# SiLU as a half of g times (1 + tanh(g/2)): one activation on ScalarE and one more pass on VectorE

## The chip, the cores and the metric

The kernel runs on one core of one Trainium2 chip. The metric is the device time of one execution in microseconds (us). In what follows PE is TensorE (matmuls, with PEld for its weight loads), DVE is VectorE, ACT is ScalarE, POOL is GpSimd and SP issues the DMAs.

## The reference

Three stages follow each other. Attention works on 4 batches of 8 heads, 576 tokens and 64 columns a head; half of the heads see a local window of 32 tokens, half a strided pattern. Its output, 2304 tokens of 512 numbers, goes through a gated layer and then through a layer with three products of which the largest counts:

```
g = x @ w_gate                       # 512 -> 1536
silu = g * (1.0 / (1.0 + np.exp(-g)))
val = x @ w_val                      # 512 -> 1536
x = (silu * val) @ w_out             # 1536 -> 512
h = np.maximum(np.maximum(x @ w1, x @ w2), x @ w3)   # 512 -> 768
return h @ w_out2                    # 768 -> 512
```

The change touches only the line `silu`.

## The kernel before

Tokens lie along the free axis. The gated layer cuts the 2304 tokens into five column blocks `c` (480, 480, 448, 448 and 448 tokens) and the 1536 hidden columns into twelve pieces `f` of 128. One pair (c, f) is called a **slot** here, numbered s = 12 c + f from 0 to 59. In slot s the PE makes the gate product `ps_g` (12 matmuls, lines 503 to 505, function `linear`), then the value product `ps_v` (12 matmuls), and then the output product of slot s-1 (`emit_out`: 12 matmuls, or 4 slower ones, line 549, issued as 8, while c is 0). Most products are made of three matmuls, of the high and low halves of their operands.

Both `ps_g` and `ps_v` come from the PSUM pool `gv`, which has two buffers. So the gate product of slot s+1 writes the buffer that held the gate product of slot s, and may begin only when the last reader of `ps_g` of slot s is done. Before the change that reader is ACT (line 523). The value product of slot s+1 waits in the same way for the DVE product of slot s (line 530), which reads `ps_v`.

The product `ht` of line 530 is then split in a high half `hh` (ACT, line 135) and a low half `hl` (POOL, line 138), from which the next output product is made; while c is 0 it is used whole.

Between the slots other work is woven in. While c is 0 each slot loads, converts (lines 158 to 163) and splits (lines 135, 138) three pieces of the weights, and does a share of the attention of block c = 1: scores (303), masked maximum and softmax (311 to 321: the exponential is line 316), transposes (326), values (340, 345, 346), and units of strided attention done on DVE or POOL (415 to 440: exponential on line 425, sums on 418 and 440). While c is 1 to 3 each slot does a share of the attention of block c+1, with its products on POOL, and of the preparation of the last layer's weights (lines 161 to 163, 195 to 198, 206, 207). At the end of block c = 4 the y blocks of the last layer are loaded and prepared (lines 135, 138, 583 to 587).

The order of instructions on each engine is set when the program is built, by a scheduler that follows a simulated timeline; each engine then works through its own list in that order and waits where an operand is not there yet. The last layer (lines 599 on) begins about 566 us after the start and takes the rest of the span.

Of the kernel before, what the change touches and what calls it, by code (L numbers as in the profile page):

```python
# [11 lines left out]
AF = mybir.ActivationFunctionType  # L12
ALU = mybir.AluOpType
# [46 lines left out]
def tile_attention_swiglu_maxout(  # L60
# [18 lines left out]
    nc = tc.nc  # L79
# [38 lines left out]
    def width(c):  # L118
        return STRIDE * (ROWS[c + 1] - ROWS[c])
# [11 lines left out]
    def split(hi, lo, src, hi_eng, lo_eng):  # L131
        if hi_eng is nc.gpsimd:
            a = nc.gpsimd.tensor_scalar(hi, src, 1.0, 1.0, ALU.mult, ALU.mult)
        elif hi_eng is nc.scalar:
            a = nc.scalar.activation(hi, src, AF.Copy)  # L135
        else:
            a = nc.vector.tensor_copy(hi, src)
        return a.ins, lo_eng.tensor_tensor(lo, src, f32(hi), ALU.subtract).ins  # L138
# [368 lines left out]
    def linear(ps, w, x, n):  # L507
        xh, xl = x
        for k in range(NK):
            ks = slice(k * 128, (k + 1) * 128)  # L510
            product(ps, w[0][:, ks], w[1][:, ks], xh[:, k, :n], xl[:, k, :n], k == 0, k == NK - 1)
# [6 lines left out]
    def emit_gate(c, f):  # L518
        n = width(c)
        ps = gv.tile([128, 512], F32, name="ps_g", tag="gv")  # L520
        linear(ps[:, :n], wt["g", f], xt[c], n)
        t = h_p.tile([128, N], F32, name="ht", tag="ht" if c or f % 2 else "hh")[:, :n]
        nc.scalar.activation(t, ps[:, :n], AF.Silu)  # L523
        return t

    def emit_val(c, f, t):
        n = width(c)
        ps = gv.tile([128, 512], F32, name="ps_v", tag="gv")
        linear(ps[:, :n], wt["v", f], xt[c], n)
        m = nc.vector.tensor_tensor(t, ps[:, :n], t, ALU.mult).ins  # L530
        if c == 0:
            hs[c, f] = (t, t)
            return
        hh = h_p.tile([128, N], F32R, name="hh")[:, :n]
        hl = h_p.tile([128, N], F32R, name="hl")[:, :n]
        last_val[:] = [m, *split(hh, hl, t, nc.scalar, nc.gpsimd)]
        hs[c, f] = (hh, hl)
# [214 lines left out]
    if True:  # L752
# [32 lines left out]
        for s, (c, f) in enumerate(slots):  # L785
# [4 lines left out]
            if work:  # L790
                weight_step()
            t = emit_gate(c, f)
            if work:
                weight_step()
            emit_val(c, f, t)
            if work:
                weight_step()
# [167 lines left out]
```

## Time and profile before

| | before |
|---|---|
| median of 3 runs | 851.76 us (849.8 to 852.48) |
| the profiled execution's own time | 850.72 us |
| its span | 848.9 us |
| busy PE, PEld | 808.7 us (95%), 712.2 us (84%) |
| busy DVE, ACT, POOL | 519.3 us (61%), 374.4 us (44%), 408.7 us (48%) |
| mean granted TensorE clock | 0.986 |

Busy time is the time in which an engine had an instruction in work. For the PE it says little: matmuls are pipelined and their ends are modelled, so a PE that is 100% busy in a stretch can still be slowed. Where the profile shows idle PE time it also names what the PE waited for.

### The profile page before, as it was taken

Reading aid. Unit: us, or ns where it says so; the run is one execution under the profiler, and the core shown is the slowest. Engines: PE = TensorE matmul, PEld = TensorE weight load, DVE = VectorE, ACT = ScalarE, POOL = GpSimd, SP = SyncE. Lnnn points to the kernel's source line nnn. Section 1 sums busy time; section 2 is a strip of 40 time slices with the busy share of each in tenths; the row PEclk is TensorE's granted clock in tenths of the full one; section 3 lists DMA queues with packets and bytes.
Section 4 is the critical chain, followed back from the end, with each engine's and each line's share of the span. In section 5 each row is a group of like instructions: output and inputs, shape, how many; then the busy total and the mean of one; then the engine's idle time right before and its main releaser. Section 6 shows DMA issues by size and latency. Waiting matters only on the chain.

```text
span 848.9 us, 12625 instructions
## 1 busy us (share of the span) xinstructions
PE 808.7 (95%) x4392; PEld 712.2 (84%) x4392; DVE 519.3 (61%) x1028; ACT 374.4 (44%) x844; POOL 408.7 (48%) x355
## 2 busy tenths in 40 slices
PE   4699988989999999999998999999999999999997
PEld 3577665768888899989887999999999899989986
DVE  3889977886576778846889552543644254524340
ACT  4987677653545353645243233432244123512220
POOL 0586566876477869746788444430313021302110
PEclk9799998999999999999999999999999999999999
DMA  8779688986766699868677997579766385654502
GB/s 231 237 237 363 202 273 294 361 261 215 246 201 217 220 311 313 297 194 274 205 226 212 350 300 271 169 291 407 252 234 217 129 284 215 220 190 147 212 1 75
DMA packets 73915, 202.72 MB, mean 239 GB/s; under 512 B 8716, under 2 KB 38472, under 8 KB 70268
## 3 DMA queue, kind: packets, MB, share of 16 engines
q1 hardware_dynamic: 73852, 201.92, 69.8%
q8 instruction: 35, 0.57, 0.3%
q14 instruction: 28, 0.23, 0.1%
HBM read 160.21 MB, written 41.68 MB: 238 GB/s over the span
## 4 chain that ended last, share of the span: by engine, by line
PE 63%; DVE 7%; POOL 3%; DMA 2%; issue 2%; ACT 2%; SPq 0%; DVEq 0%; ACTq 0%; POOLq 0%
PE ps_a L611 13%; PE ps_z L684 8%; PE ps_c L611 7%; PE ps_v L503 3%; PE ps_g L503 3%; PE ps_y L505 3%; PE ps_v L505 3%; PE ps_g L504 3%; PE ps_b L611 3%; PE ps_v L504 3%; PE ps_y L504 3%; PE ps_y L503 3%; PE ps_g L505 3%; POOL pr L415 1%; DMA wr<-wsdr 1%
## 5 line engine op out<-in xcount | busy, mean ns | idle before, releaser
L138 POOL TENSOR_TENSOR hl<-t,hh 128x384 fp32r<-128x384 f32 x36 | 37.6, 1047 | 207.5 <-ACT hh L135 160.4
L503 PE MATMUL ps_g<-xh,wh_g 128*128 128x448 f32 (+1 forms) x240 | 94.4, 394 | 10.2 <-ACT ht L523 8.1
L611 PE MATMUL ps_a<-yhT,wr 128*128 128x384 f32 x324 | 94.4, 338 | 0.6 <-ACT s L625 0.6
L503 PE MATMUL ps_v<-xh,w_v 128*128 128x448 f32 (+1 forms) x240 | 90.5, 377 | 3.5 <-DVE ht L530 3.3
L138 POOL TENSOR_TENSOR hl<-ht,hh 128x448 fp32r<-128x448 f32 (+1 forms) x48 | 60.1, 1253 | 68.1 <-ACT hh L135 60.7
L504 PE MATMUL ps_g<-xl,wh_g 128*128 128x448 f32 (+1 forms) x240 | 90.7, 378 | 0.9 <-DVE xl L346 0.9
L505 PE MATMUL ps_g<-xh,wl_g 128*128 128x448 f32 (+1 forms) x240 | 90.2, 376 | 0.0
L505 PE MATMUL ps_v<-xh,w_v 128*128 128x448 f32 (+1 forms) x240 | 89.5, 373 | 0.0
L504 PE MATMUL ps_v<-xl,w_v 128*128 128x448 f32 (+1 forms) x240 | 89.2, 372 | 0.0
L625 ACT ACTIVATE s<-ps_a 128x384 f32<-128x384 f32 x81 | 39.4, 490 | 98.4 <-PE ps_a L611 98.2
L437 POOL TENSOR_TENSOR pr<-stv,stsc 128x832 f32<-128x832 f32 (+17 forms) x42 | 67.5, 1625 | 29.2 <-DVE stsc L430 13.4
L415 POOL TENSOR_TENSOR pr<-stk,stq 128x832 f32<-128x832 f32 (+17 forms) x42 | 70.9, 1708 | 9.0 <-DVE sto L440 7.3
L505 PE MATMUL ps_y<-hh,w_o 128*128 128x448 f32 (+1 forms) x192 | 71.4, 372 | 0.0
L504 PE MATMUL ps_y<-hl,w_o 128*128 128x448 f32 (+1 forms) x192 | 71.2, 371 | 0.0
L160 POOL TENSOR_SCALAR raw<-raw 128x512 f32<-128x512 f32 x60 | 54.1, 902 | 33.4 <-ACT w L158 15.9
L503 PE MATMUL ps_y<-hh,w_o 128*128 128x448 f32 (+1 forms) x192 | 68.2, 374 | 0.0
L135 ACT ACTIVATE hh<-ht 128x448 fp32r<-128x448 f32 (+1 forms) x48 | 28.0, 584 | 88.4 <-DVE ht L530 88.4
L684 PE MATMUL ps_z<-wo2t,hh 128*128 128x512 f32 x216 | 64.8, 392 | 0.9 <-ACT osb L693 0.7
L530 DVE TENSOR_TENSOR ht<-ps_v,ht 128x448 f32<-128x448 f32 (+1 forms) x60 | 37.9, 631 | 41.9 <-PE ps_v L505 25.8
L503 PEld LDWEIGHTS ps_g<-xh,wh_g 128*128 128x128 f32 x240 | 45.8, 191 | 18.6 <-ACT ht L523 10.0
L611 PEld LDWEIGHTS ps_a<-yhT,wr 128*128 128x128 f32 x324 | 59.7, 188 | 1.6 <-ACT s L625 1.0
L163 DVE CUSTOM_DVE_ANT_0 w<-w,q 128x1024 uint16<-128x1024 uint16 x60 | 54.1, 902 | 1.7
(138 smaller groups left out, 1982.4 us busy)
## 6 DMA issues: line engine op xcount, KB each, us to landing
wr<-wsdr SPq DMA_DIRECT2D x27, 1792.0 KB, 7.5
raw<-in_w_dram SPq DMA_DIRECT2D x60, 512.0 KB, 5.3
w_v<-wvdr SPq DMA_DIRECT2D x48, 512.0 KB, 4.7
w_o<-wodr SPq DMA_DIRECT2D x48, 512.0 KB, 4.8
wsdr<-whi SPq DMA_DIRECT2D x27, 256.0 KB, 4.0
wvdr<-w_v SPq DMA_DIRECT2D x12, 512.0 KB, 4.5
wodr<-w_o SPq DMA_DIRECT2D x12, 512.0 KB, 5.8
wsdr<-w SPq DMA_DIRECT2D x18, 256.0 KB, 4.1
```

Of the source, the lines that this page charges most:

```text
L138: return a.ins, lo_eng.tensor_tensor(lo, src, f32(hi), ALU.subtract).ins
L160: nc.gpsimd.tensor_scalar(f32(hi), f32(hi), -0.0, 1.0, ALU.mult, ALU.mult)
L163: nc.vector.tensor_tensor(w, w, q, ALU.add)
L415: eng.tensor_tensor(pv, self.k[:, 0:i + 1, :], self.q[:, r:r + 1, :].to_broadcast([128, i + 1, D]), ALU.mult)
L437: eng.tensor_tensor(pv, self.v[:, :, 0:i + 1], self.sc[:, r:r + 1, 0:i + 1].to_broadcast([128, D, i + 1]), ALU.mult)
L503: nc.tensor.matmul(ps, wh, xh, start=first, stop=False)
L504: nc.tensor.matmul(ps, wh, xl, start=False, stop=False)
L505: nc.tensor.matmul(ps, wl, xh, start=False, stop=last)
L530: m = nc.vector.tensor_tensor(t, ps[:, :n], t, ALU.mult).ins
L611: nc.tensor.matmul(ps, wts[:, c, a, ks], y[k][b], start=first and k == q == 0, stop=k == 1 and q == 2, skip_group_check=True,)
L625: nc.scalar.activation(s, self.a, AF.Copy)
L684: nc.tensor.matmul(z[j], a[:, ts], w[:, f, b], start=f == q == 0, stop=f == NF2 - 1 and q == 2)
```

## The change

The activation of line 523 becomes a tanh of half of the gate product. A new DVE instruction adds 1 to it and multiplies by the gate product, which it reads from PSUM. The product with `ps_v` takes in the factor 0.5.

```
         t = h_p.tile([128, N], F32, name="ht", tag="ht" if c or f % 2 else "hh")[:, :n]
-        nc.scalar.activation(t, ps[:, :n], AF.Silu)
+        nc.scalar.activation(t, ps[:, :n], AF.Tanh, scale=0.5)
+        nc.vector.scalar_tensor_tensor(t, t, 1.0, ps[:, :n], ALU.add, ALU.mult)
         return t
...
-        m = nc.vector.tensor_tensor(t, ps[:, :n], t, ALU.mult).ins
+        m = nc.vector.scalar_tensor_tensor(t, t, 0.5, ps[:, :n], ALU.mult, ALU.mult).ins
```

All lines behind the new one move down by one: the new DVE instruction is line 524, and the product that was line 530 is line 531. In the built program the instructions that load a table into ACT (ACT_TABLE_LOAD) go from 34 to 1, the one at the start. The scheduler also places other work a little differently. Three places follow, with the rows of the DVE list; `ht<-ps_v,ht` or `ht<-ht,ps_v` is the product with the value, `ht<-ht,ps_g` the new instruction.

First the DVE around the product of slot 5, in block c = 0 (`pr` and `sto` are strided attention, `w_...` weights under conversion). Before:

```order
L430 TENSOR_TENSOR stsc<-stsc,ssum 128x36
L437 TENSOR_TENSOR pr<-stv,stsc 128x1088
L437 TENSOR_TENSOR pr<-stv,stsc 128x1152
L162 SCALAR_TENSOR_TENSOR w_992<-w_992,raw 128x512
L440 TENSOR_REDUCE sto<-pr 128x64
L530 TENSOR_TENSOR ht<-ps_v,ht 128x480
L138 TENSOR_TENSOR w_v_999<-w_964,w_v_999 128x512
```

Now:

```order
L437 TENSOR_TENSOR pr<-stv,stsc 128x1088
L437 TENSOR_TENSOR pr<-stv,stsc 128x1152
L440 TENSOR_REDUCE sto<-pr 128x64
L524 SCALAR_TENSOR_TENSOR ht<-ht,ps_g 128x480
L138 TENSOR_TENSOR w_v_1002<-w_967,w_v_1002 128x512
L162 SCALAR_TENSOR_TENSOR w_995<-w_995,raw 128x512
L440 TENSOR_REDUCE sto<-pr 128x64
L346 TENSOR_TENSOR xl<-ps_a,xh 128x2x128
L531 SCALAR_TENSOR_TENSOR ht<-ht,ps_v 128x480
```

The new instruction of slot 5 stands behind the two long products of line 437 and a sum of line 440, about where the product stood; the product has moved four rows further back.

Then the DVE of slots 44 and 45, in block c = 3 (`s_...` are sums of weights of the last layer). Before:

```order
L195 TENSOR_TENSOR s_4658<-w_4651 128x256
L440 TENSOR_REDUCE sto<-pr 128x64
L196 TENSOR_TENSOR s_4658<-s_4658,w_4567 128x256
L198 TENSOR_TENSOR s_4659<-w_4567,s_4658 128x256
L530 TENSOR_TENSOR ht<-ps_v,ht 128x448
L440 TENSOR_REDUCE sto<-pr 128x64
L207 TENSOR_TENSOR w_4567<-w_4567,whi 128x512
L207 TENSOR_TENSOR s_4658<-s_4658,whi 128x512
L440 TENSOR_REDUCE sto<-pr 128x64 x2
L530 TENSOR_TENSOR ht<-ps_v,ht 128x448
```

Now:

```order
L524 SCALAR_TENSOR_TENSOR ht<-ht,ps_g 128x448
L195 TENSOR_TENSOR s_4702<-w_4695 128x256
L196 TENSOR_TENSOR s_4702<-s_4702,w_4610 128x256
L531 SCALAR_TENSOR_TENSOR ht<-ht,ps_v 128x448
L198 TENSOR_TENSOR s_4703<-w_4610,s_4702 128x256
L440 TENSOR_REDUCE sto<-pr 128x64 x2
L207 TENSOR_TENSOR w_4610<-w_4610,whi 128x512
L207 TENSOR_TENSOR s_4702<-s_4702,whi 128x512
L524 SCALAR_TENSOR_TENSOR ht<-ht,ps_g 128x448
L440 TENSOR_REDUCE sto<-pr 128x64
L531 SCALAR_TENSOR_TENSOR ht<-ht,ps_v 128x448
L440 TENSOR_REDUCE sto<-pr 128x64
```

The product of slot 44 has moved ahead of line 198; the new instruction of slot 45 stands where two sums of line 440, which were ahead of the product, are still to come.

Last the DVE of slots 57 and 58, near the end of block c = 4 (`yl`, `yh`, `rB`, `rT` are the y blocks). Before:

```order
L530 TENSOR_TENSOR ht<-ps_v,ht 128x448
L138 TENSOR_TENSOR ylB_5626<-rB_5608,yhB_5625 128x384
L138 TENSOR_TENSOR ylB_5630<-rB_5613,yhB_5629 128x384
L583 TENSOR_TENSOR rT_5618<-rB_5610,rB_5608 128x384
L138 TENSOR_TENSOR ylT_5638<-rT_5618,yhT_5637 128x384
L586 TENSOR_TENSOR rT_5619<-rB_5615,rT_5618 128x384
L138 TENSOR_TENSOR ylB_5650<-rB_5615,yhB_5649 128x384
L587 TENSOR_TENSOR rT_5620<-rB_5613,rT_5619 128x384
L138 TENSOR_TENSOR ylT_5642<-rB_5610,yhT_5641 128x384
L530 TENSOR_TENSOR ht<-ps_v,ht 128x448 x2
```

Now:

```order
L531 SCALAR_TENSOR_TENSOR ht<-ht,ps_v 128x448
L138 TENSOR_TENSOR ylB_5684<-rB_5666,yhB_5683 128x384
L138 TENSOR_TENSOR ylB_5688<-rB_5671,yhB_5687 128x384
L584 TENSOR_TENSOR rT_5676<-rB_5668,rB_5666 128x384
L587 TENSOR_TENSOR rT_5677<-rB_5673,rT_5676 128x384
L138 TENSOR_TENSOR ylT_5696<-rT_5676,yhT_5695 128x384
L588 TENSOR_TENSOR rT_5678<-rB_5671,rT_5677 128x384
L138 TENSOR_TENSOR ylB_5708<-rB_5673,yhB_5707 128x384
L524 SCALAR_TENSOR_TENSOR ht<-ht,ps_g 128x448
L138 TENSOR_TENSOR ylT_5700<-rB_5668,yhT_5699 128x384
L531 SCALAR_TENSOR_TENSOR ht<-ht,ps_v 128x448
```

The new instruction of slot 58 stands behind all of this work on the y blocks but one subtraction of line 138.

## Rows read from the trace of the kernel before

**Rows 1.** Table loads on ACT by line: busy us, mean ns; idle before, releaser.

```profile
L523 ACT ACT_TABLE_LOAD x17 | 21.8, 1283 | 2.4 <-PE ps_g L505 2.1
...
L425 ACT ACT_TABLE_LOAD x10 | 12.8, 1283 | 9.0 <-DVE stsc L424 8.8
...
L316 ACT ACT_TABLE_LOAD x7 | 9.0, 1283 | 0.8 <-PEq L952 0.7
```

**Rows 2.** What the PE waited for, 48 to 566 us: total, times, longest.

```profile
PE ps_g L503 <- ACT ht L523: 8.1, 3, 3.3
```

**Rows 3.** Blocks c = 0, 1: length, busy PE, PEld, DVE, ACT, POOL; PEclk, DMA, GB/s.

```profile
48.65:175.77 127.12, 121.24 (x579) 86.28 (x577) 109.08 (x200) 88.20 (x176) 85.11 (x77) 0.97 0.87 293
175.77:283.71 107.94, 104.19 (x579) 88.30 (x578) 73.58 (x165) 50.12 (x119) 76.39 (x66) 0.98 0.68 224
```

**Rows 4.** Timeline of slot 51: the activation and the next gate product.

```profile
500.82 0.55 ACT L523 ACTIVATE ht<-ps_g 128x448 f32<-128x448 f32 x1 [2.52 <-PE ps_g L505]
...
505.44 0.37 PE L503 MATMUL ps_g<-xh,wh_g 128*128 128x448 f32 x1
```

**Rows 5.** Busy time of the DVE alone in slots 3 to 6 (us, busy).

```profile
75.60:108.90 33.30, 33.00 (x60) 1.00 0.78 266
```

**Rows 6.** Timeline around slot 5's DVE product: start, us, engine, line.

```profile
97.42 0.52 PE L503 MATMUL ps_g<-xh,wh_g 128*128 128x480 f32 x1
...
100.53 0.64 DVE L530 TENSOR_TENSOR ht<-ps_v,ht 128x480 f32<-128x480 f32 x1
...
101.10 0.67 DVE L138 TENSOR_TENSOR w_v<-w,w_v 128x512 fp32r<-128x512 f32 x1
```

**Rows 7.** Timeline of slots 6 and 7: ACT, DVE and the next gate product.

```profile
116.70 0.17 DVE L319 TENSOR_SCALAR stat<-stat 128x4 f32<-128x4 f32 x1 [2.02 <-ACT sm L316]
...
119.64 1.28 ACT L523 ACT_TABLE_LOAD   x1
...
120.94 0.57 ACT L523 ACTIVATE ht<-ps_g 128x480 f32<-128x480 f32 x1
...
121.54 0.66 DVE L530 TENSOR_TENSOR ht<-ps_v,ht 128x480 f32<-128x480 f32 x1 [0.76 <-ACT ht L523]
...
121.56 0.49 PE L503 MATMUL ps_g<-xh,wh_g 128*128 128x480 f32 x1 [3.29 <-ACT ht L523]
```

**Rows 8.** Timeline of slot 13: ACT, DVE and the gate product of slot 14.

```profile
186.70 1.28 ACT L523 ACT_TABLE_LOAD   x1
186.71 1.95 DVE L319 TENSOR_SCALAR stat<-stat 128x4 f32<-128x4 f32 x1 [0.49 <-ACT sm L316]
...
188.61 0.77 PE L503 MATMUL ps_g<-xh,wh_g 128*128 128x480 f32 x1 [3.17 <-ACT ht L523]
...
188.80 0.66 DVE L530 TENSOR_TENSOR ht<-ps_v,ht 128x480 f32<-128x480 f32 x1
```

**Rows 9.** Timeline of slot 45: DVE, and the gate product of slot 46.

```profile
460.84 2.27 DVE L440 TENSOR_REDUCE sto<-pr 128x64 f32<-128x960 f32 x2
...
461.06 0.37 PE L503 MATMUL ps_g<-xh,wh_g 128*128 128x448 f32 x1
...
463.03 0.61 DVE L530 TENSOR_TENSOR ht<-ps_v,ht 128x448 f32<-128x448 f32 x1
```

**Rows 10.** Timeline of slot 58: DVE, gate and value product of slot 59.

```profile
556.57 0.37 PE L503 MATMUL ps_g<-xh,wh_g 128*128 128x448 f32 x1
...
558.10 0.55 DVE L138 TENSOR_TENSOR ylT<-rB,yhT 128x384 fp32r<-128x384 f32 x1
...
558.57 0.61 DVE L530 TENSOR_TENSOR ht<-ps_v,ht 128x448 f32<-128x448 f32 x1
...
559.24 0.47 PE L503 MATMUL ps_v<-xh,w_v 128*128 128x448 f32 x1
```

**Rows 11.** Two stretches after PE stalls (columns as rows 3; 0.66 and 0.83 are PEclk).

```profile
140.00:150.00 10.00, 9.65 (x26) 6.21 (x27) 7.21 (x23) 7.76 (x21) 6.21 (x7) 0.66 0.96 330
185.00:195.00 10.00, 6.83 (x26) 5.47 (x25) 7.23 (x9) 5.72 (x14) 8.80 (x8) 0.83 0.24 88
```

## The prediction

> **What bounds the kernel now.** I read the grouped instructions of ACT first. A function that is not in the table ACT holds costs a table load, and SiLU and the exponentials of attention push each other out: 34 loads of 1.283 us, 17 ahead of the activation of line 523 and 17 ahead of an exponential [rows 1]. That is 43.6 us of ACT, and the reader should ask at once who waits for ACT. The PE's waits answer: between 48 and 566 us it waited 8.1 us for the activation that frees `ps_g`, in three places, 3.3 us at most [rows 2]. So the 43.6 us are nearly all beside other work, and no more than about 8 us of them can come back in this way.
>
> Next the stretches. In block c = 0 the DVE is busy 109.08 of 127.12 us (86%) and ACT 88.20 (69%); in c = 1 the DVE has 73.58 of 107.94 us [rows 3]. The change takes work from the second of these engines and gives work to the first. The reader should see the margin too: in a quiet slot the activation ends at 501.37 us and the next gate product starts at 505.44, because the PE has the value product and an output product to do in between. So `ps_g` is free 4.07 us before it is needed [rows 4]. A new reader of `ps_g` costs nothing as long as it is done inside that margin.
>
> Then the timeline of the DVE where it is fullest: from 75.6 to 108.9 us, slots 3 to 6, it is busy 33.00 of 33.30 us [rows 5]. There the DVE, not the PE, paces the slots, and what is put on its list pushes all that stands behind it.
>
> **The change part by part.** *Removed:* 33 table loads, 42.3 us of ACT. Only those on the way to a wait count. *Unchanged:* the tanh is an activation of the same shape, and the product with the factor 0.5 is the old product with a constant more; I take both at the old length, since a constant adds no element (0 taken; 60 x 0.02 us, the difference between two such products in [rows 6, 7], as the other end). *Added:* 60 DVE instructions over 448 or 480 columns, one operand in PSUM and one in SBUF, the shape of the product of line 530. This operation on such operands has no row; the nearest is that product, 0.64 us long with the next DVE instruction starting 0.57 us after it [rows 6]. I take 0.57 us where more work is queued and 0.65 us where someone waits for the end; 60 of them are 34 us of DVE.
>
> *Moved:* the freeing of `ps_g`. Before, ACT did it; now the new DVE instruction does, and it waits in the DVE's list behind whatever the scheduler put there. Queued behind it are the product with `ps_v`, on which the split and the next output product hang, and the weight conversions. So in each slot two DVE instructions must be in time instead of one, and the first of them about one value product earlier. This is the wait that takes the place of the table loads. I go through the places where the DVE is late.
>
> *Slot 5.* Before, the product ran at 100.53 us behind the line 437 and 440 work, while the next gate product had already started at 97.42, since ACT had freed the buffer [rows 6]. In the new list the new instruction stands about where the product stood, with one conversion (line 162, some 1 us) moved behind it. New instructions of slots 3 and 4 push it by 2 x 0.57. So it starts near 100.53 - 1.0 + 1.1 = 100.6 and ends near 101.3: the gate product of slot 6 starts 3.9 us later than before.
>
> *Slot 7* gives most of that back. The gate product of slot 8 waited 3.29 us at 121.56 for the activation, behind a table load at 119.64 [rows 7]. The PE, 3.9 us later, uses up that wait and is 3.9 - 3.3 = 0.6 us later at slot 8. The DVE allows this: its list ran to 120.78 (121.54 less 0.76 of waiting), gets four new instructions (2.3 us) in the meantime and loses a 2.02 us wait for exponentials [rows 7], so its new instruction starts at about 121.0 and ends at 121.7, before the PE's 122.2. I take **+0.6**, bounds -3.3 (the DVE is never late) and +3.9 (the wait is not used up).
>
> *Slots 8 to 12.* Five new instructions, 2.9 us of DVE in a block where it is busy 86% [rows 3]. Between nothing and 2.9 us I take the half, **+1.4**.
>
> *Slot 13.* The gate product of slot 14 started at 188.61 after 3.17 us of waiting for the activation, behind the load at 186.70. That load goes. But in the new list the new instruction stands behind a scaling of the softmax (line 319) that took 1.95 us from 186.71, and the old product started behind it at 188.80 [rows 8]. The new one then ends at 188.80 + 0.65 = 189.45: **+0.8**. Bounds: -1.3 if that scaling takes a short 0.17 us as in [rows 7] (189.45 less 1.8 is 187.7, 0.9 us earlier than before, and a little less clock is lost) and +0.8.
>
> *Slots 44 and 45.* The DVE is a long list here; in the new order two sums of line 440, 2.27 us for both, have moved behind the new instruction of slot 45. The old product started at 463.03, so the new instruction starts at 463.03 - 2.27 + 0.57 (that of slot 44) = 461.3 and ends at 461.95, against a gate product that started at 461.06 [rows 9]: **+0.9**. Bounds: 0 and +3.2 (none of the sums helps).
>
> *Slot 58.* The old product started at 558.57; of what was ahead of it only one subtraction (0.47 us to the next start) has moved behind the new instruction. That ends at 558.57 - 0.47 + 0.61 = 558.7 against a gate product that started at 556.57. The value product of slot 59, which followed at 559.24, comes at 558.7 + 2.67 (a gate product, between these two rows) = 561.4 [rows 10]: **+2.1**, bounds 0 and +2.6.
>
> *Everywhere else* the new instruction lies inside the margin of 4 us [rows 4]. The last layer is not touched.
>
> The sum is 0.6 + 1.4 + 0.8 + 0.9 + 2.1 = 5.8 us on the profiled execution's own 850.72 us, so **856.5 us**. The median of the runs shown is 851.76, 1.04 above that execution; a median of the changed kernel may stand as far above 856.5, which the range holds.
>
> *A rule against this change.* The new instruction starts its successor 0.57 us after its own start, a little under its length [rows 6]; I counted that. The Trainium skill (VectorE: DVE Perf Modes, Rules for kernel authors) says of chained DVE work to minimize the number of operations, since each pays its pipeline drain whatever is fused. By the same page's figure for a two-operand fp32 operation, (N + 151)/0.96 ns, an estimate is 0.66 us a piece at 480 columns, which would make the half of five instructions 1.6 instead of 1.4 us.
>
> **The rivals.** *Relief, faster.* The waits for the activation go and the DVE is always in time. It needs the new instruction to end within 4 us of the gate product in slots 5, 44, 45 and 58 too, where the old list says 2 to 4 us later [rows 6, 9, 10]; the order could help if real waits for exponentials on the DVE (2.02 us at 116.70, [rows 7]) shrink by the loads ahead of them. Price: 8.1 us [rows 2] and the low clock behind the stall at 185 us, (1 - 0.83) x 10 = 1.7 us [rows 11]: 850.7 - 9.8 = 841 us; with half of it 846. It decides from the point where the new instruction of slot 5 ends before 97.4.
> What a load costs bears on this rival. In the rows the activation follows 1.30 us after the load's start [rows 7]. The Trainium skill (ScalarE: Activation LUTs, What ACT_TABLE_LOAD costs) adds a drain and gives about 2.66 us for every switch, and names exp and tanh as one set. By it the 33 switches would be 88 us of ACT; the trace does not show such a drain, and the waits, which are measured, stay what they are.
>
> *Even.* Half of the waits come back and half of the new ones come: 850.7 + (5.8 - 8.1)/2 = 849.6. For it speaks that slot 5's delay is paid out of a wait that goes; against it that slot 58 has no wait to give back.
>
> *The DVE becomes the bound of c = 0.* All twelve instructions lie on the path, 12 x 0.57 = 6.8 us in place of 0.6 + 1.4; with the other terms (3.8) and one more stall of about 3.4 us of low clock as at 140 to 150 us, (1 - 0.66) x 10 [rows 11], 864.7. For it speaks 86% of busy time, against it the 18 us in which the DVE of that block still waits [rows 3].
>
> That the loads stay is excluded by the built program, which has one.
>
> **How the numbers follow.** About 0.3%, 2.6 us, is what a measurement of this kernel can tell from no change. The forecast (853.4 to 860) has 0.42, the DVE bound (860 to 867) 0.13, both slower: 0.55. Even (848 to 853.3) has 0.22. Relief (841 to 848) has 0.23. The range from 846 to 866 leaves out the better half of relief and little above: 0.15. The likeliest case's own range is 853.4 to 860.
>
> **What would show it.** ACT has one table load and is some 42 us less busy; the DVE some 34 us more. The PE's waits for ACT at its gate products are gone, and waits for the new DVE instruction (`ht`, line 524) stand in their place: about 4 us at slot 6, others near slots 14, 46 and 59. Blocks c = 1 and c = 2 change by less than 2 us. If instead the PE has no wait at line 503 for the DVE, my step on slot 5 is wrong, and relief is right; if c = 0 is 7 us or more longer, the DVE has become its bound. Waits of the PE for other engines, weights above all, would make me wrong in a way that is not in the cases.

## The result, and the profile after

The changed kernel takes 859.21 us (median of 5 runs, 857.32 to 861.69), the kernel before, run beside it, 849.8 us (848.37 to 852.48). The recorded ratio is 1.0086, with an interval from 1.0058 to 1.0114 (these two medians alone give 1.011, within it): it became slower. The two profiled executions took 859.57 and 850.72 us, 8.85 us apart; that is the difference which the steps below divide up.

The page's busy times of the changed kernel, with its span ahead:

```profile
span 857.7 us, 12675 instructions
...
PE 813.2 (95%) x4392; PEld 714.6 (83%) x4392; DVE 557.1 (65%) x1088; ACT 331.2 (39%) x811; POOL 408.2 (48%) x355
```

ACT is 43 us less busy (374.4 before) and the DVE 38 us more (519.3 before). The groups by line answer to [rows 1], first on ACT:

```profile
L316 ACT ACT_TABLE_LOAD x1 | 1.3, 1283 | 0.7 <-PEq L953 0.7
...
L531 DVE SCALAR_TENSOR_TENSOR ht<-ht,ps_v 128x448 f32<-128x448 f32 (+1 forms) x60 | 37.7, 629 | 20.7 <-PE ps_v L505 19.3
L524 DVE SCALAR_TENSOR_TENSOR ht<-ht,ps_g 128x448 f32<-128x448 f32 (+1 forms) x60 | 37.6, 626 | 33.3 <-ACT ht L523 33.3
```

One load is left of 34. The new instruction takes 626 ns, as long as the product beside it. What the PE waited for between 48 and 575 us answers to [rows 2]:

```profile
PE ps_g L503 <- DVE ht L524: 14.2, 9, 4.3
PE ps_a L303 <- DVE xl L346: 2.4, 2, 2.1
PE ps_v L503 <- DVE ht L531: 2.4, 2, 1.7
PE ps_a L326 <- DVE sm L321: 1.3, 1, 1.3
```

No gate product waits for ACT any more. In place of 8.1 us for the activation stand 14.2 us for the new DVE instruction, in nine places. The timeline shows the two waits in the full stretch of the DVE (81.25 us, for the new instruction of slot 3, and 85.83 us, for the product of slot 3), and the places of the forecast, which answer to [rows 6] to [rows 10]:

```profile
79.29 1.34 DVE L415 TENSOR_TENSOR pr<-stk,stq 128x1152 f32<-128x1152 f32 x1
80.56 0.64 DVE L524 SCALAR_TENSOR_TENSOR ht<-ht,ps_g 128x480 f32<-128x480 f32 x1
...
81.25 0.49 PE L503 MATMUL ps_g<-xh,wh_g 128*128 128x480 f32 x1 [1.55 <-DVE ht L524]
...
85.83 0.48 PE L503 MATMUL ps_v<-xh,w_v 128*128 128x480 f32 x1 [1.68 <-DVE ht L531]
...
97.25 0.55 ACT L523 ACTIVATE ht<-ps_g 128x480 f32<-128x480 f32 x1
...
100.85 0.64 DVE L524 SCALAR_TENSOR_TENSOR ht<-ht,ps_g 128x480 f32<-128x480 f32 x1
...
101.29 0.45 PE L340 MATMUL ps_a<-loct 96*64 96x64 f32 x8
...
101.68 0.48 PE L503 MATMUL ps_g<-xh,wh_g 128*128 128x480 f32 x1
...
120.01 0.17 DVE L319 TENSOR_SCALAR stat<-stat 128x4 f32<-128x4 f32 x1 [0.96 <-ACT sm L316]
...
122.75 0.64 DVE L524 SCALAR_TENSOR_TENSOR ht<-ht,ps_g 128x480 f32<-128x480 f32 x1
...
122.97 0.60 PE L326 MATMUL ps_a<-cst,sm 128*60 128x128 f32 x4 [1.30 <-DVE sm L321]
...
123.44 0.48 PE L503 MATMUL ps_g<-xh,wh_g 128*128 128x480 f32 x1
...
188.67 2.33 POOL L437 TENSOR_TENSOR pr<-stv,stsc 128x1088 f32<-128x1088 f32 x1 [0.37 <-DVE sto L440]
...
189.14 1.88 DVE L319 TENSOR_SCALAR stat<-stat 128x4 f32<-128x4 f32 x1 [0.55 <-ACT sm L316]
...
191.16 0.64 DVE L524 SCALAR_TENSOR_TENSOR ht<-ht,ps_g 128x480 f32<-128x480 f32 x1
...
191.85 0.77 PE L503 MATMUL ps_g<-xh,wh_g 128*128 128x480 f32 x1 [4.27 <-DVE ht L524]
...
457.66 0.47 PE L503 MATMUL ps_v<-xh,w_v 128*128 128x448 f32 x1 [0.70 <-DVE ht L531]
...
465.42 0.47 PE L503 MATMUL ps_g<-xh,wh_g 128*128 128x448 f32 x1 [2.42 <-DVE ht L524]
...
561.73 1.37 DVE L587 TENSOR_TENSOR rT<-rB,rT 128x384 f32<-128x384 f32 x1 [2.13 <-DMA rB<-ydr]
...
565.23 0.61 DVE L524 SCALAR_TENSOR_TENSOR ht<-ht,ps_g 128x448 f32<-128x448 f32 x1
...
565.89 0.47 PE L503 MATMUL ps_g<-xh,wh_g 128*128 128x448 f32 x1 [1.84 <-DVE ht L524]
```

Each time the new instruction is late on the DVE. In slot 5 ACT is done with `ps_g` at 97.80 us, but the new instruction starts 3.05 us later, behind the strided attention on the DVE. The gate product of slot 6 starts 0.19 us after its end, but the row shows no wait there: the PE had attention's products (line 340) to make until 101.74 us, so its own work and the release ended within 0.3 us of each other. In slot 58 the instruction is held up by work on a y block whose DMA the DVE itself waited 2.13 us for: a transfer that has nothing to do with `ps_g` now delays its release.

A wait of the PE can have a second price. These are two stretches from a gate product to the next, slot 14 and slot 46, of the kernel before (length, busy times, then the granted clock as a share of 2.4 GHz):

```profile
188.61:196.60 7.99, 7.99 (x32) 6.82 (x33) 4.70 (x7) 2.92 (x5) 5.62 (x6) 0.81 0.01 4
461.06:467.10 6.04, 6.04 (x32) 5.45 (x31) 4.60 (x6) 2.54 (x6) 6.04 (x4) 1.00 1.04 327
```

and of the changed one:

```profile
191.85:201.00 9.15, 9.15 (x36) 7.73 (x37) 5.27 (x6) 3.25 (x6) 5.12 (x5) 0.74 0.03 5
465.42:472.90 7.48, 7.48 (x30) 6.58 (x31) 6.36 (x9) 2.79 (x6) 7.48 (x6) 0.77 0.83 249
```

The PE is busy throughout in all four, but behind the waits of 4.27 and 2.42 us it ran part of the time at the lower level, 1.2 GHz, and the slots took 1.16 and 1.44 us longer than before. Not all of the 1.16 is clock: the changed order has 36 matmuls in that slot instead of 32, and at full clock the two would be 0.74 x 9.15 = 6.8 and 0.81 x 7.99 = 6.5 us, which leaves 0.9 us for the clock. Nor has every wait this price: behind the 1.84 us at slot 59 the granted clock is 1.00.

### The profile page after: what moved, and what is told of

It reads as the page before. It is cut to its first block, busy times and chain, and to the rows that moved or that the text cites. A ratio compares the mean times of both kernels' runs of the same rounds, so it can differ in the third digit from the quotient of the medians.

```text
span 857.7 us, 12675 instructions
## 1 busy us (share of the span) xinstructions
PE 813.2 (95%) x4392; PEld 714.6 (83%) x4392; DVE 557.1 (65%) x1088; ACT 331.2 (39%) x811; POOL 408.2 (48%) x355
## 4 chain that ended last, share of the span: by engine, by line
PE 60%; DVE 10%; POOL 4%; DMA 2%; issue 2%; ACT 1%; SPq 0%; DVEq 0%; POOLq 0%; ACTq 0%
PE ps_a L612 13%; PE ps_z L685 8%; PE ps_c L612 7%; PE ps_g L503 3%; PE ps_g L504 3%; PE ps_g L505 3%; PE ps_b L612 3%; PE ps_v L503 3%; PE ps_v L505 3%; PE ps_v L504 3%; PE ps_y L503 3%; PE ps_y L504 3%; PE ps_y L505 3%; POOL pr L415 3%; DVE stsc L418 1%
## 5 line engine op out<-in xcount | busy, mean ns | idle before, releaser
L503 PE MATMUL ps_g<-xh,wh_g 128*128 128x448 f32 (+1 forms) x240 | 95.9, 400 | 16.4 <-DVE ht L524 14.2
L503 PE MATMUL ps_v<-xh,w_v 128*128 128x448 f32 (+1 forms) x240 | 90.8, 378 | 2.4 <-DVE ht L531 2.4
L505 PE MATMUL ps_v<-xh,w_v 128*128 128x448 f32 (+1 forms) x240 | 91.1, 380 | 0.0
L505 PE MATMUL ps_y<-hh,w_o 128*128 128x448 f32 (+1 forms) x192 | 71.2, 371 | 0.0
L503 PE MATMUL ps_y<-hh,w_o 128*128 128x448 f32 (+1 forms) x192 | 64.9, 375 | 0.0
L524 DVE SCALAR_TENSOR_TENSOR ht<-ht,ps_g 128x448 f32<-128x448 f32 (+1 forms) x60 | 37.6, 626 | 33.3 <-ACT ht L523 33.3
L523 ACT ACTIVATE ht<-ps_g 128x448 f32<-128x448 f32 (+1 forms) x60 | 32.9, 549 | 67.4 <-PE ps_g L505 60.5
```

Of the source, the lines that this page charges most:

```text
L503: nc.tensor.matmul(ps, wh, xh, start=first, stop=False)
L505: nc.tensor.matmul(ps, wl, xh, start=False, stop=last)
L523: nc.scalar.activation(t, ps[:, :n], AF.Tanh, scale=0.5)
L524: nc.vector.scalar_tensor_tensor(t, t, 1.0, ps[:, :n], ALU.add, ALU.mult)
```

## The experiments

The theory, A, is that of the prediction: the loss comes from the place of the release, `ps_g` being freed from a place far back in the DVE's list. The rival, B, is that 37.6 us more work on the DVE cost the time wherever they stand. Beside both stands the question what the 33 loads were worth. Each kernel is compared with the kernel before on the same chip (851.5 to 851.9 us there; the changed kernel would be at about 859.0 by its ratio, 7.3 us above it, with an interval from 4.9 to 9.7).

**The two halves of the change.** The first kernel keeps the tanh and leaves out the new instruction, the second keeps it but goes back to SiLU as the function.

```diff
         nc.scalar.activation(t, ps[:, :n], AF.Tanh, scale=0.5)
-        nc.vector.scalar_tensor_tensor(t, t, 1.0, ps[:, :n], ALU.add, ALU.mult)
```

> The tanh stands alone: the new VectorE instruction is left out, so the hidden layer becomes tanh(g/2) times half of the value instead of SiLU times the value. The table loads are gone and ScalarE frees ps_g as before the change. Theory A (the loss comes from ps_g being freed late, behind the list of the DVE): only the relief is left, so 841 to 847 us, with the PE's 8.1 us of waits for the activation down to under 2 us. Theory B (the loss comes from 38 us more DVE work): the same 841 to 847 us. Theory C (the loss comes from the order into which the scheduler put everything else once the loads' instruction was another): no gain, 850 us or more.

```diff
-        nc.scalar.activation(t, ps[:, :n], AF.Tanh, scale=0.5)
+        nc.scalar.activation(t, ps[:, :n], AF.Silu)
         nc.vector.scalar_tensor_tensor(t, t, 1.0, ps[:, :n], ALU.add, ALU.mult)
```

> SiLU on ScalarE with its 34 table loads stays, and the new DVE instruction is there all the same, reading ps_g (the hidden layer becomes (SiLU(g)+1) times g/2 times the value). Theory A: both the loads and the DVE's list now lie between the gate product and the freeing of ps_g; where the list is late the loads add little, so 860 to 865 us, less than after plus the whole relief. Theory B: cost and relief simply add, so after plus what the kernel with the tanh alone gains, some 864 to 868 us.

The tanh alone took 847.74 us, ratio 0.9945 (0.9925 to 0.9965), just above the 841 to 847 that A and B both expected. Apart from the loads it lists the instructions of the kernel before in the same order on every engine, so the 4.0 us are what the loads cost there. The PE's waits between 48 and 575 us:

```profile
PE ps_v L503 <- DVE ht L530: 5.2, 2, 3.3
PE ps_a L303 <- DMA loct<-in_st1k_dram: 3.8, 1, 3.8
PE ps_g L503 <- ACT ht L523: 3.5, 3, 1.7
```

Of the 8.1 us for the activation 3.5 stay; what goes there partly comes up again as a wait of attention for its DMA.

SiLU with the new instruction took 867.77 us, 1.0181 (1.0155 to 1.0208). It has 34 loads and otherwise the order of the changed kernel, so under that order the loads cost about 867.8 - 859.0 = 8.8 us, twice as much. That lies in the range of B, but not by its sum (859.0 + 4.0 = 863.0): cost and relief do not simply add, and A's 860 to 865 is missed too. Its PE waited for the new instruction 15.7 us:

```profile
PE ps_g L503 <- DVE ht L524: 15.7, 10, 3.4
```

That is only 1.5 us more than the changed kernel's 14.2, so why the loads cost twice as much here is not shown. The changed kernel lies 859.0 - 847.7 = 11.3 us above the tanh alone: that is the new instruction together with the other order that the scheduler makes of it.

**The new instruction off PSUM.** It multiplies the tanh instead of `g` (another function), and ACT is the last reader of `ps_g` again.

```diff
-        nc.vector.scalar_tensor_tensor(t, t, 1.0, ps[:, :n], ALU.add, ALU.mult)
+        nc.vector.scalar_tensor_tensor(t, t, 1.0, t, ALU.add, ALU.mult)
```

> The new DVE instruction stays, 60 times, but multiplies by the tanh itself in SBUF instead of by ps_g (the hidden layer becomes (tanh+1) times tanh times half of the value). ScalarE frees ps_g again; the DVE has as much to do as in the changed kernel. Theory A: the PE's waits for the DVE at the gate products are gone and the time is 843 to 851 us. Theory B: the DVE has the same work, so 857 us or more.

857.77 us, 1.007 (1.0043 to 1.0097). It tells less than it was meant to, since the instruction itself changed:

```profile
L524 DVE SCALAR_TENSOR_TENSOR ht<-ht 128x448 f32<-128x448 f32 (+1 forms) x60 | 63.6, 1060 | 19.7 <-ACT ht L523 19.5
...
PE ps_v L503 <- DVE ht L531: 14.6, 7, 4.5
```

With both operands in SBUF it takes 1060 instead of 626 ns. Its waits moved from `ps_g` to `ps_v`. For theory A it is no test: the work became 26 us longer.

**The same work on `ps_v`.** The added instruction stands beside the product and reads `ps_v` instead of `ps_g` (the value enters squared, the gate not at all); ACT frees `ps_g`.

```diff
         linear(ps[:, :n], wt["v", f], xt[c], n)
+        nc.vector.scalar_tensor_tensor(t, t, 1.0, ps[:, :n], ALU.add, ALU.mult)
         m = nc.vector.scalar_tensor_tensor(t, t, 0.5, ps[:, :n], ALU.mult, ALU.mult).ins
```

> The added DVE instruction keeps its length of 0.63 us (one operand in PSUM, one in SBUF, unlike the experiment that multiplied in SBUF and made it 1.06 us long), but stands behind the value product and reads ps_v, right ahead of the old product (the hidden layer becomes (tanh+1) times half of the value squared). ScalarE frees ps_g. DVE work is that of the changed kernel. Theory A (ps_g freed late): 847 to 853 us against a kernel before at about 851, waits of the PE at the gate product for the DVE gone. Theory B (38 us more DVE work, wherever it stands): 857 us or more, with the waits now at the value product.

**The same place with less work.** The new instruction still frees `ps_g`, but works on 8 columns, or on half of them; the others keep the bare tanh.

```diff
-        nc.vector.scalar_tensor_tensor(t, t, 1.0, ps[:, :n], ALU.add, ALU.mult)
+        nc.vector.scalar_tensor_tensor(t[:, :8], t[:, :8], 1.0, ps[:, :8], ALU.add, ALU.mult)
```

> The added DVE instruction stays in its place and frees ps_g, but takes only 8 of the 448 or 480 columns (the other columns of the hidden layer keep the tanh alone), some 0.16 us instead of 0.63: the DVE has about 28 us less to do than in the changed kernel. Theory A: the release still hangs on the list of the DVE, so at least two thirds of the loss stay: 855 us or more. Theory B: the loss goes with the work, so within 3 us of the kernel with the tanh alone: 847 to 851 us.

> The added instruction takes half of the columns (224 or 240; the other half of the hidden layer keeps the tanh alone), about 0.39 us instead of 0.63, between the 0.15 us of the run with 8 columns (844.3) and the changed kernel (about 859). If the loss grows with the length of the instruction: 850 to 854 us. If what costs is that the release stands in the DVE's list, with a jump as soon as the list is longer than the margin: 855 or more, or still 847 or less.

On `ps_v` it took 854.19 us, 1.0025 (1.0005 to 1.0044); 8 columns 844.3, 0.9921 (0.9902 to 0.994); half of them 849.57, 0.997 (0.9949 to 0.9991). The new instruction takes 154 ns at 8 columns and 387 at half. The first lies between what A and B expected (847 to 853; 857 or more), the second below both (855 or more; 847 to 851), and the third just under the 850 to 854 of a loss that grows with the length. So theory A in the form that the place alone makes the loss falls: with the same release and 0.15 us a slot the kernel is faster than before, and no slower than the tanh alone (0.9921 against 0.9945, with intervals that overlap). And B alone doesn't do either: the full work on `ps_v` is about 5 us cheaper than on `ps_g`. The waits of the PE for `ps_v` in the first and for `ps_g` in the second:

```profile
PE ps_v L503 <- DVE ht L531: 9.1, 6, 3.0
```

```profile
PE ps_g L503 <- DVE ht L524: 6.5, 5, 1.9
```

The start of each slot's gate product, against the kernel before, divides the time by place. The columns give how much each stretch grew or shrank in us, from the timelines (the last row is the shift at slot 59, from the unrounded times):

| stretch | tanh alone | 8 columns | half | changed kernel | on `ps_v` |
|---|---|---|---|---|---|
| to slot 6 | -0.6 | +0.3 | +1.8 | +4.3 | +6.0 |
| 6 to 13 | +1.7 | -6.1 | -4.1 | -2.2 | -4.5 |
| 13 to 15 | -2.8 | 0.0 | +2.9 | +2.3 | -0.6 |
| 15 to 42 | -1.0 | -2.5 | -4.5 | -0.2 | -5.3 |
| 42 to 57 | 0.0 | 0.0 | -1.2 | +2.2 | +6.6 |
| 57 to 59 | 0.0 | +1.6 | +2.8 | +2.9 | 0.0 |
| sum | -2.7 | -6.8 | -2.5 | +9.3 | +2.4 |

Each column comes from one execution, and executions of the kernel before lay up to 9 us apart on one chip (847.7 to 856.7 us), so a row of a microsecond or less says little by itself; of the later blocks the timelines repeat well (the changed kernel and SiLU with the new instruction, of one order, keep their shift within 0.02 us from slot 28 to 45).

Neither theory holds everywhere, and both hold somewhere. Up to slot 6 it is the work: the loss grows with the length of the instruction, and is there on `ps_v` as well. At slots 58 and 59 it is the place: 8 columns already cost half of it, and on `ps_v` it is gone. It looks the same at slots 13 to 15, where the release by ACT gives 0.6 to 2.8 us and the release by the DVE loses up to 2.9. At slots 42 to 57 the work on `ps_v` costs most, 6.6 us. One caution: the scheduler orders each of these kernels differently. At slot 9 the order of 8 columns puts attention's scores behind the output product, and at half the PE waits for them 0.3 us only; a stall of 1.8 to 3.8 us with low clock behind it that the other four have is not there. Granted clock from 140 to 150 us, 8 columns:

```profile
140.00:150.00 10.00, 8.03 (x33) 5.34 (x31) 8.77 (x28) 8.62 (x24) 6.52 (x7) 1.00 0.98 382
```

The changed kernel has 0.73 in these 10 us, the kernel before 0.66 [rows 11]. From the gate product of slot 9 to that of slot 12 this is worth 2.9 us to 8 columns and 0.8 to half. How the 11.3 us divide between work and place to the last microsecond is therefore open.

**The order.** One kernel gives the tanh and the new instruction the scheduler's high priority; the other makes each slot's later work stand behind the new instruction in the program's order. Both have all instructions of the change.

```diff
+        with tc.high_priority():
+            nc.scalar.activation(t, ps[:, :n], AF.Tanh, scale=0.5)
+            nc.vector.scalar_tensor_tensor(t, t, 1.0, ps[:, :n], ALU.add, ALU.mult)
```

> The same instructions as the changed kernel; the tanh and the new instruction only have a higher priority for the scheduler, which gives another order of the lists with no edge added. It shows how much the order by itself is worth: within 2 us of the changed kernel (857 to 861) if the order hardly matters; 2 to 5 us faster if the place of the new instruction does; further off if the order of the rest is worth as much as the change itself.

```diff
+            with tc.issue_after(last_gate[0]):
+                if work:
+                    weight_step()
+                emit_val(c, f, t)
...
```

> The changed kernel, all of its arithmetic, with an order for the DVE: conversions and attention work that a slot issues behind its gate product may not stand ahead of the new instruction of that slot. In slot 5 the new instruction then stands ahead of the two long products of line 437. Theory A: the new instruction is less late, the 3.9 us at slot 5 shrink below 1.5 us, and the time falls to 851 to 856 us. Theory B: same instructions on every engine, so as the changed kernel, 857 to 860 us, or more for the weight conversions that come later.

The first took 854.62 us, 1.004 (1.002 to 1.006), 4.4 us below the changed kernel, with 8.3 us of waits for the new instruction. In its profiled execution slots 42 to 57 shrink by 1.9 us against the kernel before where the changed kernel grows by 2.2, and slots 57 to 59 grow by 1.1 instead of 2.9. Up to slot 6 it loses as the changed kernel does, 5.6 against 4.3 us. A gain of 2 to 5 us was what was expected if the place matters; by these rows the place of the instruction, with what else the order moves, is worth some 6 us at the late slots and nothing at the early ones. The second took 863.96, 1.0142 (1.0111 to 1.0172), outside the 851 to 856 of A, with 10.3 (in an execution of 867.87 us, the slowest of six):

```profile
PE ps_g L503 <- DVE ht L525: 10.3, 10, 3.6
PE ps_a L303 <- DMA loct<-in_lock_dram: 3.7, 1, 3.7
PE ps_a L447 <- DVE sto L440: 3.1, 2, 2.1
PE ps_a L303 <- DMA loct<-in_st1k_dram: 2.9, 1, 2.9
```

Both shorten the waits for the new instruction. The second holds up what starts attention's transfers (two of them are issued at 71.55 and 76.36 us instead of 54.27 and 68.17), and the PE waits for those. But at slot 24 it is only 1.2 us behind the changed kernel; 5.6 us are lost from there to slot 36 and 5.4 from slot 47 to 50, against 4.1 won from 42 to 47, and what loses them is open. The same instructions in three orders lie between 854.6 and 864.0 us, further apart than the 7.3 us that the change costs.

**Less work on a full DVE.** The steps of the attention of block c = 1 that go through `eng` (the products of lines 415 and 437, and the scaling of the softmax, line 321) are made on POOL instead of the DVE, in the changed kernel and, as a control, in the kernel before.

```diff
-        eng = nc.vector if c == 1 else nc.gpsimd
+        eng = nc.gpsimd
```

> The changed kernel with the attention of block c = 1 (products of lines 415 and 437, scaling of line 321) on POOL instead of the DVE, some 8 us less for the DVE in slots 2 to 14, where it is fullest. If the loss in blocks c = 0 and 1 comes from a DVE that is full there (both theories in their forms for that place), the 4 us lost by slot 6 shrink below 2 and the time falls by 2 to 4 us against the changed kernel, to 855 to 857; if it comes from the place in the list alone, no change, 859.

> The kernel before with the same move of the attention of c = 1 to POOL: the control. Where the DVE has room, as before the change, its 8 us buy little: within 2 us of the kernel before, 850 to 853 (slower if POOL becomes late with it). Only what the changed kernel gains beyond this is the change's own pressure on the DVE.

862.1 us, 1.0125 (1.0104 to 1.0146), against 858.56, 1.0079 (1.006 to 1.0098). The move itself costs 6.6 us. On top of it the change costs 3.5 us instead of 7.3, with a DVE that has 14 us less to do (543.1 us busy). Both times lie above what was expected (855 to 859; 850 to 853). By place, the 4.3 us that the change costs up to slot 6 are 0.0 between these two, and slots 57 to 59 still cost 3.4 us. That agrees with B in c = 0 and with A at the end, but the intervals are wide enough for no difference in the sum, and the control is a worse kernel, itself 6.6 us late at slot 6 with the PE waiting for weights there: up to slot 6 a hint only.

**Slack at the release.** The pool of `ps_g` and `ps_v` gets three buffers, taken from attention's, again in both kernels.

```diff
-    gv = sub(one, "gv", 2, space=PS)
-    att = sub(one, "att", 2, space=PS)
+    gv = sub(one, "gv", 3, space=PS)
+    att = sub(one, "att", 1, space=PS)
```

> The changed kernel with three buffers for the gate and value products (pool gv) instead of two, and one instead of two for the attention's (pool att). ps_g then has one product more (2.6 us) before its buffer is wanted again. If lateness of the release is what turns the longer list of the DVE into lost PE time, the waits of the PE for the DVE at gate and value products (16.6 us in the changed kernel) fall below 6 us, and the time falls by at least 4 us against what the same change of pools does to the kernel before. If the DVE is simply full, nothing is won beyond that control.

> The kernel before with the same pools: the control, which shows what the single attention buffer costs. Its waits for ACT and DVE at gate and value products (11.4 us) mostly go, the attention's products wait more: 846 to 856 us.

884.01 us, 1.0379 (1.0354 to 1.0405), with the change and 888.33, 1.0435 (1.0409 to 1.046), without. Both lose over 32 us, where the control was expected at 846 to 856: with one buffer the PE waits for attention instead. The order of the two is turned round: here the change gains 4.3 us. The PE's waits with the change name attention:

```profile
PE ps_a L303 <- DVE xl L346: 5.5, 2, 3.2
PE ps_g L503 <- ACT xh L458: 4.2, 3, 2.2
PE ps_y L550 <- DVE w L163: 4.0, 1, 4.0
```

No gate product waits for the new instruction. But the 4.3 us are no measure of the release. From slot 12 to 13 alone the changed kernel gains 7.6 us on its control, where the PE waits for attention in both, and no run has the tanh alone with these pools, so what the loads cost there is not known. At slot 6 the change is 4.7 us behind its control with three buffers as well, and 0.5 at slot 7.

The end of block c = 4 has no attention, and there the pair can be compared. The DVE's list at slots 57 and 58 is the same as with two buffers, with a wait of 1.87 us for a y block, and the new instruction of slot 58 is as late:

```profile
589.74 0.37 PE L503 MATMUL ps_g<-xh,wh_g 128*128 128x448 f32 x1
...
591.68 0.61 DVE L524 SCALAR_TENSOR_TENSOR ht<-ht,ps_g 128x448 f32<-128x448 f32 x1
```

The gate product of slot 59 starts 1.94 us ahead of it, without a wait, and the two slots take 14.61 us against 14.64 in the control, where two buffers lost 2.9. So at this place the loss needs both, a late instruction and a release that is due within a slot. Up to slot 6 it is the work. No kernel that does the whole computation was faster than the one before.

## Why the prediction was right

The forecast was slower, 856.5 us with the sum at +5.8; measured were 859.21 and +8.85. By its own steps, each as the shift of a gate product's start against the kernel before:

- *Slot 5*, +3.9 forecast: +4.3 (97.42 to 101.68 us). The new instruction started at 100.85 us instead of 100.6. But the PE did not lose the time there, and the agreement of the two numbers is in part luck: 3.3 us had come by the gate product of slot 5 already, with the waits of 1.55 and 1.68 us at 81.25 and 85.83, and the last 1.0 comes in slot 5 with no idle PE time, attention's products of line 340 being in it now. The wait of about 4 us at slot 6 that was to show the step is not there. The DVE's list was rightly added up over slots 3 to 5, and its lateness was put at the end of the stretch where the PE met it at the start. The work on `ps_v` costs as much by there (6.0 us), so the release of `ps_g` is not what makes this loss.
- *Slot 7* gives most of it back, +0.6 left: +1.9 was left. The wait for the activation was used up as forecast, but the DVE's list was later: the wait for exponentials shrank to 0.96 us instead of vanishing, and the new instruction started at 122.75, not 121.0. What the PE waited for is another instruction of that list, the scaling of line 321 (1.30 us at 122.97).
- *Slots 8 to 12*, +1.4: they gained 0.2 on top of the 1.9, so that the sum at slot 13 was +2.1 against a forecast of +2.0. That two misses cancel (1.3 too little at slot 7, 1.2 too much here) is luck, and no merit of the half that was taken between nothing and 2.9.
- *Slot 13*, +0.8, which was also the step's upper bound: +1.1 at slot 14, behind the scaling of line 319 that the step named (1.88 us long again). Then came 1.2 us in slot 14 itself, which no term held: the wait grew from 3.17 to 4.27 us, the clock behind it fell from 0.81 to 0.74 (0.9 us), and four more matmuls stood in the slot.
- *Slots 44 and 45*, +0.9: the gate product of slot 46 came only 0.1 us later than the shift of slot 42. The new wait of 2.42 us stands there, and the wait of the value product in slot 45 shrank by 2.6, from 3.33 to 0.70. But slot 46 then took 1.44 us longer, at a clock of 0.77 instead of 1.00, and by slot 57 the stretch had lost 2.2.
- *Slot 58*, +2.1: the gate product of slot 59 came 2.1 us later, as forecast. A second wait of 0.63 us a slot earlier, for the new instruction of slot 57, adds 0.8; the step had no term for that instruction.
- *Everywhere else*: from the gate product of slot 12 to that of slot 24 block c = 1 grew by 1.6 us, block c = 2 by 0.8, under the 2 us that were named. The last layer gave 0.5 back.

The direction, the engine and the places were right; the sum was 3 us short. The mechanism, a release that waits in the DVE's list, is shown at slots 58 and 59, and the waits name it at slots 14 and 46; up to slot 6 it is the DVE's work that costs, whichever buffer it frees. The mis-sized terms are those of slot 13 and of slots 44 and 45: they priced the late instruction, and not the clock that the PE loses behind a longer wait, 0.9 + 1.4 = 2.3 us of the 3. Slot 58 explains 0.8, and the rest cancels.

Of the rivals, *relief* was real, and less than half as large as it was priced: 4.0 us by the tanh alone, not 9.8, since 3.5 of the 8.1 us of waits stay and others come up. *The DVE becomes the bound of c = 0* did not happen: the block gave 2.2 of the 4.3 us of slot 6 back by slot 13. The length of the new instruction, taken from the product with `ps_v`, was right (626 ns against 631). The rule of the Trainium skill (VectorE: DVE Perf Modes, Rules for kernel authors), to minimize the number of chained operations, points the right way here: one more operation cost 11.3 us beside the tanh alone. The trace adds that the cost depends on who waits for it: with a third buffer the 2.9 us at slots 57 to 59 are gone.

## What to carry to other kernels

Work that moves off a busy engine is worth what the waits behind it cost, not its length: 42 us of table loads were worth 4, and under another order 9. Before a DVE instruction becomes the one that frees a PSUM buffer, look in its list at each place where it would stand behind long work, or work that waits for a DMA, and compare its end with the margin to the next writer; a stall that it makes costs its own length and, where the PE's clock falls behind it, more (here 1.4 us behind a wait of 2.4). And reordering the same instructions can weigh as much as the change, so compare kernels with equal orders where there are any.

## What the runs showed of the hardware

- The same DVE operation took 626 ns on average with one operand in PSUM and 1060 ns with both in SBUF, from 605 to 2711 ns (median 894). The Trainium skill (GPSIMD Engine Reference, Specifications) says that GpSimd shares its SBUF interfaces with VectorE and that they contend when a DVE instruction has two SBUF inputs; the traces agree. With both operands in SBUF the 20 instructions with no POOL instruction beside them took 605 to 659 ns, and the 40 with one 1275 ns on average. With one operand in PSUM they took 602 to 655 ns without and 605 to 656 with POOL beside them. No run took POOL's work away.
- The price of the new instruction is not in proportion to its length: against the tanh alone, 154 and 387 ns a slot came out 3.4 us faster and 1.8 us slower, both within the intervals, and 626 ns 11.3 us slower. The orders differ, so this is no property of the instruction alone.
- A scaling of 128x4 numbers on the DVE (line 319) took 0.17 us in one slot and 1.88 in another of the same execution. It sat on the path at slot 13 in both kernels. Over both traces the 25 such scalings (line 319) with no POOL instruction beside them took 0.14 to 0.17 us, and the ten that took over 1 us each ended 0.02 to 0.03 us behind the end of a POOL instruction; in slot 13 that is the strided product of line 437, from 188.67 to 191.00 us. By these ends the long ones waited for POOL, and such waiting counts as busy time of the DVE; the new instruction of slot 13 stood behind one. No run took that product away, so this is read from the traces and not tried.
